# One bank tile for the pairs of heads, kept for the whole kernel, and a state update that writes 48 rows for each head

## The chip, the cores and the metric

The kernel runs on one core of one Trainium2 chip. The metric is the device time of one execution in microseconds (us), the median of several runs. For the kernel before, three runs took 460.72, 461.08 and 461.09 us, so the median is 461.08 us.

## The reference: what is computed

A gated linear attention feeds a feed-forward block that has no nonlinearity but one product. Cut to what matters:

```python
# q, k, v, f_logit: (batch 4, heads 8, sequence 768, head size 48), float32
f = 1.0 / (1.0 + np.exp(-f_logit))
for t in range(S):
    state = f[:, :, t, :, None] * state + np.einsum('bhd,bhe->bhde', k[:, :, t], v[:, :, t])
    y[:, :, t] = np.einsum('bhd,bhde->bhe', q[:, :, t], state)
x = y.transpose(0, 2, 1, 3).reshape(B * S, H * D)      # 3072 x 384
a = x @ w1                                             # 384 x 1024
b = x @ w2
h = a * b @ w3                                         # 1024 x 1024
out = h @ w_out                                        # 1024 x 384
```

## The kernel before, in words

The attention works on 24 units u of 128 positions (`C` = 128), six to each batch entry. The eight heads stand in four pairs hp. In the tiles of q, k and the gates the even head of a pair (par 0) has partitions 0 to 47 and the odd head (par 1) partitions 64 to 111. Partitions 48 to 63 between them are padding. The memsets in `setup` make the padding of q and k zero. `rows(par)` is the slice of 48 partitions of one head; `R` is 112, both heads with the padding between.

For each unit VectorE scans the gates forward (L529) and backward (L551) and scales q (L545) and k (L559). Scaled k is turned on TensorE (`turn`, L596) and copied to the tile `kt` by ScalarE (L730). From unit 2 on (`NPE` = 2) the units are cut into two halves of 64 positions (`W`), and the work of a unit on TensorE is this:

- `pairs` (L582): products of k and q, 16 matmuls of 64 x 64 outputs, into the left half (256 columns) of each of the two banks of the tile `pa`.
- `update` (L689): the product of turned k and v, which is what the unit adds to the state. For each pair hp, each half and each par there is one matmul, 16 in all, with 64 positions as the contraction and 48 columns of v as the moving operand. They write columns 256 to 447 of the two banks of the same `pa`, the first half's sums into bank 0 and the second's into bank 1. For par 0 the stationary operand has 64 columns of `kt` (head and padding), for par 1 it has 48 (`w` in L688), so that rows 0 to 111 are written without a gap. The last unit of each batch entry (u = 5, 11, 17, 23) does the first half alone, 8 matmuls.
- `values` (L656) and `from_state` (L675): the outputs of the unit, into `py`.

From unit 4 on (`SOLO` = 4) these are interleaved in one visit of TensorE, the function `visit` in `rest`: half of the values of unit u, the pairs of u + 1, the other half of the values, the part from the state of u, and last the update of u + 1. What reads `pa`: ScalarE copies the pairs (L706), GpSimd masks the copy in place (L712), and VectorE reads rows 0 to 111 of the update (L760, L762 and L765, the function `middle`) to make the state after each half. Of the state only the 48 rows of each head are used (L676, L677).

`pa` comes from the pool `ps`, which has one buffer for each name. `pairs` asks for the tile in each unit, so each unit's `pa` is a new tile at the old place, and its first write waits for everything that touched the tile before it.

Around the visits the same TensorE queue runs the products of weights and the feed-forward block: L901, L997, L1152 and L1470, 128 x 128 stationary operands with 192 to 384 columns moving. `idle` (L402) puts in matmuls without use. The order on every engine is set when the program is built: class `Plan` lists the tasks by written-out costs, due times and a limited number of banks, and the tasks are emitted in that order. The costs in the plan are not touched by the change. At run time each engine takes its instructions in that order and waits on semaphores.

Of the kernel before, what the change touches and what calls it, by code (L numbers as in the profile page):

```python
# [36 lines left out]
F32 = mybir.dt.float32  # L37
# [7 lines left out]
B, H, S, D = 4, 8, 768, 48  # L45
P = 128
# [13 lines left out]
NQ = HP * C  # L60
# [9 lines left out]
W = C // 2  # L70
# [220 lines left out]
def rows(par):  # L291
    return slice(64 * par, 64 * par + D)
# [3 lines left out]
def ranged(ctx, tc, q, k, f_logit, v, w1, w2, w3, w_out, out, ident, w12, wc, left):  # L296
# [15 lines left out]
    ps = pairing.enter_context(tc.tile_pool(name="ps", bufs=1, space=PSUM))  # L312
# [48 lines left out]
    found = {}  # L361
# [202 lines left out]

    def pairs(u):
        s = st[u]
        s["pa"] = ps.tile([P, 2, NQ], F32, name="pa")
        if u < NPE:
            for hp in range(HP):
                cols = slice(hp * C, hp * C + C)  # L570
                for par in range(2):
                    nc.tensor.matmul(
                        s["pa"][:, par, cols], lhsT=s["K"][rows(par), cols], rhs=s["Q"][rows(par), cols],
                        start=True, stop=True,
                    )
            return

        for hp in range(HP):
            for half in range(2):
                cols = slice(hp * C + half * W, hp * C + half * W + W)  # L580
                for par in range(2):
                    nc.tensor.matmul(  # L582
                        s["pa"][half * W : half * W + W, par, hp * W : hp * W + W],
                        lhsT=s["K"][rows(par), cols], rhs=s["Q"][rows(par), cols], start=True, stop=True,
                    )
# [94 lines left out]
    def update(u):  # L680

        s = st[u]
        s["pd"] = [s["pa"][0:R, half, HP * W : HP * W + HP * D].rearrange("p (h d) -> p h d", d=D) for half in range(2)]
        for hp in range(HP):
            for half in range(1 if u % NCH == NCH - 1 else 2):
                for par in range(2):
                    h = 2 * hp + par
                    w = 64 if par == 0 else D  # L688
                    nc.tensor.matmul(  # L689
                        s["pd"][half][64 * par : 64 * par + w, hp],  # L690
                        lhsT=s["kt"][half * W : half * W + W, hp, 64 * par : 64 * par + w],
                        rhs=s["v"][half * W : half * W + W, h * D : h * D + D], start=True, stop=True,
                    )

# [45 lines left out]
    def begin(u):  # L740

        def emit():
            pairs(u)
            update(u)

        t = tk[u]
        t["a"] = t["s"] = plan.add(
            "PE", 1.1, emit, [t["q"], t["k"], t["e"], t["lv"]] + past(u, 1, "m", "d"), need(u) - 999, slack=0.8,
        )
        paired(u)  # L750
# [20 lines left out]
    def rest(u):  # L771
        s, t = st[u], tk[u]
        opens, closes = u % NCH == 0, u % NCH == NCH - 1
        n0 = need(u)
        if u < NPE:
            t["a"] = plan.add("PE", 1.1, lambda: pairs(u), [t["q"], t["k"]] + past(u, 1, "m"), n0 - 1000)
            turning(u)
            paired(u)
# [6 lines left out]
        else:  # L785
# [4 lines left out]
            def visit():  # L790
                s["py"] = ps.tile([P, 2, NQ], F32, name="py")
                values(u, 1)
                if more:
                    pairs(u + 1)
                values(u, 0)
                from_state(u)
                if more:
                    update(u + 1)
# [822 lines left out]
    for item in EARLY:  # L1621
        if item in "ABCD":
            half, which = divmod("ABCD".index(item), 2)
# [394 lines left out]
```

## Time and profile before

| | before |
|---|---|
| median of three runs | 461.08 us |
| lowest and highest run | 460.72 and 461.09 us |
| span of the profiled execution, first to last instruction | 459.2 us |
| DVE (VectorE) busy in it | 370.7 us (81%) |
| ACT (ScalarE) busy | 211.7 us (46%) |
| POOL (GpSimd) busy | 66.3 us (14%) |
| DMA mean rate | 150 GB/s |
| granted TensorE clock | 1.000 |

The page gives the profiled execution's own time as its span alone, 459.2 us. It is 1.9 us under the median of the runs, which take in what lies ahead of the first instruction and behind the last. TensorE has two rows in the profile: PE is the matmuls, PEld the weight loads that run beside them. A 32-bit matmul of this kernel leaves two records of each (a transpose one), so 16 matmuls stand as x32. In a form such as `64*48 64x48` the first pair is the stationary operand (64 rows of contraction, 48 columns) and the second the moving one (64 rows, 48 columns). A line such as L689 is a line of the kernel; "f", "l", "pa" and "py" are banks. A releaser behind an arrow is what ended the idle time ahead of an instruction. "PEldq" and "PEq" are TensorE's sequencer, which passes the instructions on.

### The profile page before, as it was taken

What the parts mean: (1) busy time and instruction counts of PE and PEld (TensorE: products, weight loads), DVE (VectorE), ACT (ScalarE), POOL (GpSimd) and SP (SyncE); (2) the same over time, 40 slices, a digit from 0 to 9 for tenths busy, and PEclk for the clock granted to TensorE, in tenths of its full rate; (3) what the DMA queues carried; (4) which work ended last, traced back from release to release, by engine and by line L of the source; (5) the groups of instructions that cost most, each with busy time, mean ns of one, the idle gap of its engine ahead of it and who ended that gap; (6) DMA issues with size and microseconds to landing.
All of it is one profiled execution on the core that took longest, in us unless ns stands there. A gap on an engine that the chain in (4) does not pass through costs nothing.

```text
span 459.2 us, 11789 instructions
## 1 busy us (share of the span) xinstructions
PE 450.8 (98%) x4792; PEld 394.6 (86%) x4792; DVE 370.7 (81%) x651; ACT 211.7 (46%) x473; POOL 66.3 (14%) x90
## 2 busy tenths in 40 slices
PE   7999999999999999999999999999999999999996
PEld 6788886666899888889999888899899988889996
DVE  8997899999898999989999699896659466767641
ACT  3565344332233453543322256665665666665300
POOL 9331000121222531132222000000000000000000
PEclk9999999999999999999999999999999999999999
DMA  6997898833236664356322602436365522333111
GB/s 180 283 314 239 299 334 299 264 110 104 71 90 196 198 192 128 105 158 177 98 76 63 164 0 93 137 119 211 132 199 177 192 72 93 92 93 91 36 68 40
DMA packets 43309, 68.75 MB, mean 150 GB/s; under 512 B 5217, under 2 KB 28386, under 8 KB 42226
## 3 DMA queue, kind: packets, MB, share of 16 engines
q1 hardware_dynamic: 43250, 67.95, 48.2%
q8 instruction: 39, 0.64, 0.6%
q14 instruction: 20, 0.16, 0.1%
HBM read 58.88 MB, written 9.04 MB: 148 GB/s over the span
## 4 chain that ended last, share of the span: by engine, by line
PE 95%; DVE 1%; SPq 1%; DMA 1%; issue 0%; POOL 0%; POOLq 0%; DVEq 0%
PE f L901 24%; PE l L1152 15%; PE f L997 13%; PE f L1152 12%; PE f L1470 9%; PE l L901 9%; PE py L656 3%; PE pa L582 2%; PE pa L689 2%; PE f L596 2%; PE py L675 2%; PE f L402 1%; SPq L495 1%; DMA ab<-in_k_dram 1%; DVE K L559 0%
## 5 line engine op out<-in xcount | busy, mean ns | idle before, releaser
L712 POOL TENSOR_SCALAR_AFFINE_SELECT A<-A 64x512 f32<-64x512 f32 (+1 forms) x46 | 43.9, 955 | 110.5 <-ACT A L706 108.3
L1470 PE MATMUL f<-place 128*128 128x384 f32 x128 | 42.4, 487 | 0.0
L901 PE MATMUL f<-xt,w 128*128 128x256 f32 x192 | 42.1, 380 | 0.0
L901 PEld LDWEIGHTS f<-xt,w 128*128 128x128 f32 x192 | 36.3, 190 | 5.0
L1470 PEld LDWEIGHTS f<-place 128*128 128x128 f32 x128 | 23.9, 190 | 15.5
L901 PE MATMUL f<-place 128*128 128x192 f32 x176 | 31.9, 327 | 0.0
L997 PE MATMUL f<-xt,w 128*128 128x256 f32 x120 | 31.3, 380 | 0.0
L529 DVE TENSOR_TENSOR_SCAN fwd<-gate,floor 112x512 f32<-112x512 f32 x24 | 30.0, 1251 | 1.3 <-ACT gate L521 0.3
L551 DVE TENSOR_TENSOR_SCAN bwd<-gate,back 112x512 f32<-112x512 f32 x24 | 30.4, 1267 | 0.7
L901 PEld LDWEIGHTS f<-place 128*128 128x128 f32 x176 | 28.9, 190 | 0.4 <-issue 0.2
L848 ACT ACTIVATE ys<-py 112x512 f32<-112x512 f32 x22 | 13.1, 596 | 33.3 <-PE py L675 31.5
L997 PEld LDWEIGHTS f<-xt,w 128*128 128x128 f32 x120 | 22.5, 190 | 2.9
L901 PE MATMUL f<-wc,ab 128*128 128x192 f32 x128 | 23.6, 328 | 0.0
L1406 ACT ACTIVATE place<-place 128x512 f32<-128x512 uint32 (+2 forms) x24 | 21.2, 885 | 4.6 <-DMA place<-in_w_dram 4.0
L812 POOL TENSOR_TENSOR G<-lasts,gate 112x4 f32<-112x4 f32 x20 | 11.7, 586 | 75.1 <-ACT lasts L534 30.4
L901 PEld LDWEIGHTS f<-wc,ab 128*128 128x128 f32 x128 | 21.2, 190 | 0.3
L521 ACT ACTIVATE gate<-f 112x512 f32<-112x512 f32 x22 | 13.9, 632 | 16.0 <-DMA f<-in_f_logit_dram 7.0
L901 PE MATMUL l<-place 128*128 128x192 f32 x112 | 19.8, 326 | 0.0
L656 PEld LDWEIGHTS py<-A,vt 64*64 64x64 f32 (+1 forms) x672 | 13.3, 127 | 7.3 <-issue 6.5
L997 PE MATMUL f<-place 128*128 128x256 f32 x72 | 19.1, 386 | 0.0
L901 PEld LDWEIGHTS l<-place 128*128 128x128 f32 x112 | 18.5, 190 | 0.1
L656 PE MATMUL py<-A,vt 64*64 64x64 f32 (+1 forms) x672 | 18.0, 223 | 0.2
(288 smaller groups left out, 1066.7 us busy)
## 6 DMA issues: line engine op xcount, KB each, us to landing
place<-in_w_dram SPq DMA_DIRECT2D x21, 512.0 KB, 5.4
A<-in_w_dram SPq DMA_DIRECT2D x19, 512.0 KB, 4.0
place<-in_w_dram SPq DMA_DIRECT2D x8, 1024.0 KB, 6.2
q<-in_q_dram SPq DMA_DIRECT2D x46, 96.0 KB, 2.7
vt<-in_v_dram SPq DMA_DIRECT2D x23, 192.0 KB, 3.2
out_dram<-o SPq DMA_DIRECT2D x23, 192.0 KB, 2.9
k<-in_k_dram SPq DMA_DIRECT2D x44, 96.0 KB, 2.4
yt<-ys SPq DMA_DIRECT2D x44, 96.0 KB, 2.7
```

Source lines behind the costliest of these rows:

```text
L521: nc.scalar.activation(gate[u % 2][:, 0:NQ], fu, AF.Sigmoid)
L529: nc.vector.tensor_tensor_scan(s["P"], gate[u % 2][:, 0:NQ], floor, 0.0, ALU.mult, ALU.max)
L551: nc.vector.tensor_tensor_scan(s["R"][:, ::-1], gate[u % 2][:, NQ:0:-1], back[:, ::-1], 0.0, ALU.mult, ALU.max)
L656: done = nc.tensor.matmul(y_block(u, hp, par, half)[p0 : p0 + w], lhsT=s["v"][half * W : half * W + W, h * D : h * D + w], rhs=s["A"][half ...
L712: nc.gpsimd.affine_select(out=a, in_=a, pattern=pattern, compare_op=ALU.is_ge, fill=0.0, base=0, channel_multiplier=-1,)
L812: nc.gpsimd.tensor_tensor(s["G"], lasts[:, u], heads(gate[(u + 1) % 2][:, 0:NQ])[:, :, 0], ALU.mult)
L848: nc.scalar.activation(ys, py, AF.Copy, accum_out=ysum[:, u : u + 1])
L901: nc.tensor.matmul(out_, lhsT=lhs[i], rhs=rhs[i], start=start and i == 0, stop=i == len(lhs) - 1, skip_group_check=True,)
L997: nc.tensor.matmul(q[nm][:, which * TH : which * TH + TH], lhsT=lhs[i](which), rhs=rhs[i], start=start and which == 0 and i == 0, stop=i = ...
L1152: nc.tensor.matmul(banks[g, c][:, which * TH : which * TH + TH], lhsT=lhs, rhs=x_node(a), start=first and which == 0, stop=True, skip_grou ...
L1406: nc.scalar.activation(part_.bitcast(F32), part_, AF.Copy, bias=2.0, scale=2.0**-51)
L1470: nc.tensor.matmul(w3s["p", jc], lhsT=w3s[jc][:, kc * P : kc * P + P], rhs=wos[:, kc], start=(kc == 0), stop=(kc == KF - 1),)
```

## The change

It does two things. The tile `pa` is asked for once, in the first unit, and kept in `found`; all later units write to that one tile. And `update` takes `rows(par)` for both heads: the stationary operand has 48 columns for par 0 too, and rows 48 to 63 of `pa` are not written by the update any more. They keep what the pairs of the first two units left there, which filled all 128 rows; VectorE's reads of rows 0 to 111 go on as they were.

```diff
     def pairs(u):
         s = st[u]
-        s["pa"] = ps.tile([P, 2, NQ], F32, name="pa")
+        if "pa" not in found:
+            found["pa"] = ps.tile([P, 2, NQ], F32, name="pa")
+        s["pa"] = found["pa"]
...
                 for par in range(2):
                     h = 2 * hp + par
-                    w = 64 if par == 0 else D
                     nc.tensor.matmul(
-                        s["pd"][half][64 * par : 64 * par + w, hp],
-                        lhsT=s["kt"][half * W : half * W + W, hp, 64 * par : 64 * par + w],
+                        s["pd"][half][rows(par), hp],
+                        lhsT=s["kt"][half * W : half * W + W, hp, rows(par)],
                         rhs=s["v"][half * W : half * W + W, h * D : h * D + D], start=True, stop=True,
```

The order of the work on every engine stays; line numbers from 567 on move by two, and from 689 on by one. What moves is shown at two places. The first is TensorE's queue at the pairs and the update of unit 3 (the sizes here are those of the output, rows x columns; the name behind "waits" is the engine whose semaphore is waited for). Before:

```order
L675 MATMUL py<-Q,A 48x64 x7
L582 MATMUL pa<-Q,K 64x64 [waits DVE_49,PE_49]
L582 MATMUL pa<-Q,K 64x64 x15
L689 MATMUL pa<-place,kt 64x48 [waits DMAHW6_49,Activation_49]
L689 MATMUL pa<-place,kt 48x48
L689 MATMUL pa<-place,kt 64x48
L689 MATMUL pa<-place,kt 48x48
```

Twelve more rows of the update follow, 64 and 48 rows high by turns. The same place after the change:

```order
L677 MATMUL py<-Q,A 48x64 x7
L584 MATMUL pa<-Q,K 64x64 [waits DVE_49]
L584 MATMUL pa<-Q,K 64x64 x15
L690 MATMUL pa<-place,kt 48x48 [waits DMAHW6_49,Activation_49]
L690 MATMUL pa<-place,kt 48x48 x15
```

All 16 matmuls of the update are now 48 rows high, and the pairs no longer wait for TensorE's own earlier write of the tile. In 13 units such a wait goes; where it was the second wait of an instruction it had a sequencer instruction of its own, and 12 of these go from TensorE's queue.

The second place is ScalarE's copy of the pairs in the same unit. Before:

```order
L848 ACTIVATE ys,ysum<-py 112x2x2x128 [waits PE_49]
L1406 ACTIVATE place<-place 128x512 [waits DMAHW2_49]
L706 COPY A<-pa 128x512 [waits PE_49,Pool_49]
```

After the change:

```order
L849 ACTIVATE ys,ysum<-py 112x2x2x128 [waits PE_49]
L1407 ACTIVATE place<-place 128x512 [waits DMAHW2_49]
L707 COPY A<-pa 128x512 [waits DVE_49,PE_49,Pool_49]
```

Seven such copies now also wait for a VectorE instruction, the read of the update one unit earlier (L765 before). For four of them that takes one more sequencer instruction on ScalarE. VectorE, GpSimd and the DMA queues have the same instructions and the same waits as before.

## The prediction

> **What bounds the kernel now.** First the page: the busy shares, and the chain of work that ended last, by engine.
>
> ```profile
> PE 450.8 (98%) x4792; PEld 394.6 (86%) x4792; DVE 370.7 (81%) x651; ACT 211.7 (46%) x473; POOL 66.3 (14%) x90
> PE 95%; DVE 1%; SPq 1%; DMA 1%; issue 0%; POOL 0%; POOLq 0%; DVEq 0%
> ```
>
> TensorE is busy for 98% of the span and carries 95% of the chain, so what TensorE no longer does is a gain unless it then waits. The view of PE's waits is short:
>
> ```profile
> engine line waited for: us in total, times, longest us
> PE f L402 <- DVE floor L425: 1.7, 1, 1.7
> PE py L596 <- DVE K L559: 0.7, 1, 0.7
> PE pa L689 <- issue: 0.6, 1, 0.6
> PE f L596 <- DVE K L559: 0.4, 1, 0.4
> ```
>
> None of these lies in the long middle or in the feed-forward at the end. Now one visit in the timeline (start, length, engine, line, operation, shape, records):
>
> ```profile
> 146.95 0.56 PEld L582 LDWEIGHTS pa<-Q,K 48*64 48x64 f32 x32
> 147.64 0.31 PEld L675 LDWEIGHTS py<-Q,S 48*48 48x48 f32 x16
> 147.87 0.31 PEld L675 LDWEIGHTS py<-Q,A 48*48 48x48 f32 x16
> 148.09 0.56 PEld L689 LDWEIGHTS pa<-vt,kt 64*48 64x48 f32 x32
> 148.14 0.64 PE L689 MATMUL pa<-vt,kt 64*48 64x48 f32 x32
> 148.71 0.62 PEld L901 LDWEIGHTS f<-place,ab 128*128 128x128 f32 x4
> ```
>
> The update takes 0.62 us from its first weight load (148.09) to that of the next full-width matmul (148.71). The timeline names a merged group by its first shape; both widths are in it. So the decisive view is the groups with shapes kept apart, from 40 to 260 us, which holds the updates of units 4 to 23 (busy time is the union of the records; mean ns of one):
>
> ```profile
> L689 PE MATMUL pa<-vt,kt 64*64 64x48 f32 x288 | 12.4, 216 | 0.0
> L689 PE MATMUL pa<-vt,kt 64*48 64x48 f32 x288 | 11.0, 206 | 0.0
> L689 PEld LDWEIGHTS pa<-vt,kt 64*64 64x64 f32 x288 | 10.9, 135 | 0.0
> L689 PEld LDWEIGHTS pa<-vt,kt 64*48 64x48 f32 x288 | 9.4, 120 | 0.0
> ```
>
> The two widths are the same number of matmuls, with the same 64 rows of contraction and the same 48 columns moving, and they run side by side on the two column halves of the array. The wide ones take longer as a stream. That they also end later is seen in a window just ahead of the next full-width matmul, from 148.69 to 148.70, in which one group alone is left:
>
> ```profile
> L689 PE MATMUL pa<-vt,kt 64*64 64x48 f32 x4 | 0.3, 218 | 0.0
> ```
>
> So the 64-wide stream sets the end of the update, and the change makes it 48 wide.
>
> **The change part by part.** *Width of the update.* The 288 records of a width are 16 updates of 16 and four of 8, 20 updates. The streams differ by 12.4 - 11.0 = 1.4 us in matmuls and 10.9 - 9.4 = 1.5 us in loads: 0.07 to 0.075 us for each update. I take 0.075, as the stream of loads is what paces them (the moving operand is equal), so 20 x 0.075 = 1.5 us. The shorter last matmul (206 against 216 ns) is within the union and isn't counted again.
>
> This price assumes that two 48-wide streams run as fast as one beside a 64-wide one, which the trace doesn't show. From below: the nearest rows with 48 x 48 on all tiles are the two L675 groups, 16 matmuls from 147.64 to 147.87 + 0.31 = 148.18, or 0.54 us of loads against the update's 0.56; that would be 0.02 us each (their moving operand has 64 columns, which is why I don't take it). From above: the window shows the narrow stream over by 148.69 and the wide one ends at 148.14 + 0.64 = 148.78, at least 0.09 us later; I bound it by 0.10. A loss has no instruction to come from, since the counts are equal.
>
> The Trainium skill ("TensorE: Matmul & The Clock Gate", section "LDWEIGHTS (loading the stationary operand)") says that a weight load's time goes with its columns, columns / 1.2 in ns. An estimate from that page: 53 against 40 ns, 13 ns for each of eight loads in a row on a tile, 0.107 us an update, 2.3 us for 22 updates, 458.7 us. The rows have 135 against 120 ns, a difference of 15 ns, and agree in sign and about in size; the streams themselves show less, and I keep to them.
>
> *Units 2 and 3.* Unit 3's update stalls in its middle:
>
> ```profile
> 28.61 0.27 PE L689 MATMUL pa<-place,kt 64*48 64x48 f32 x3
> 29.47 0.67 PE L689 MATMUL pa<-place,kt 64*48 64x48 f32 x29 [0.59 <-issue]
> 208.16 0.78 PE L689 MATMUL pa<-vt,kt 64*48 64x48 f32 x32
> q8 instruction: 39, 0.64, 0.6%
> ```
>
> Nothing that the profile shows is waited for there. The 39 packets of instructions on q8 against 4792 + 4792 TensorE records make some 246 instructions a packet, so I read it as TensorE waiting for its own code. Unit 17's update (208.16) lasts 0.14 us longer than the one above, a small one of the kind. What unit 2 saves (at 23 us) runs into the large stall, whose end the code sets: 0. The rest of unit 3's update comes behind it: 0.075 us.
>
> *The waits that go.* The waits on TensorE's own write each had 51 ns of the sequencer:
>
> ```profile
> L582 PEldq EVENT_SEMAPHORE  x11: 51/51/51, 27.9 to 247.9; - x11
> L582 PE MATMUL pa<-Q,K 48*64 48x64 f32 x640 | 12.9, 218 | 0.0
> ```
>
> The matmuls of the pairs had no idle time ahead of them from 40 to 260 us (the 0.0 at the end): the write waited for is a whole unit old, and the sequencer runs ahead of the array behind the values. I take 0; the other end is 11 x 0.051 = 0.56 us.
>
> *The waits that come.* Four more sequencer instructions on ScalarE at most 0.2 us, on an engine 46% busy. Behind the copy stand ScalarE's later instructions and GpSimd's mask, for which the next visit's L656 waits. The closest case that I find:
>
> ```profile
> 158.93 1.53 POOL L712 TENSOR_SCALAR_AFFINE_SELECT A<-A 64x512 f32<-64x512 f32 x1
> 161.39 0.45 PE L656 MATMUL py<-A,vt 64*64 64x64 f32 x16
> ```
>
> The mask ended at 160.46, 0.93 us ahead of its use. The VectorE read that is newly waited for belongs to the unit before, and the pairs themselves still wait for VectorE to be past it, so it costs 0. Without that cover it would be 0.05 us four times.
>
> *Does the gain run into another wait?* TensorE gets up to 1.6 us ahead by unit 23. Its tightest wait after 40 us is on sums of VectorE:
>
> ```profile
> 124.67 0.42 DVE L943 TENSOR_TENSOR ab<-f,ab 128x256 f32<-128x256 f32 x1 [0.91 <-PE f L901]
> 125.86 0.69 DVE L1268 TENSOR_TENSOR place<-place,ab 128x512 f32<-128x512 f32 x1
> 126.70 1.54 PE L901 MATMUL f<-place 128*128 128x192 f32 x8
> ```
>
> TensorE starts 0.15 us after the sum. But that chain began with VectorE waiting 0.91 us for TensorE, so it moves along. The other close one is scaled k (L559) ahead of its turning:
>
> ```profile
> 168.54 0.69 DVE L559 TENSOR_TENSOR K<-k,bwd 112x512 f32<-112x512 f32 x1
> 169.99 0.60 PE L596 MATMUL f<-ident,K 112*128 112x112 f32 x4
> 167.48 0.69 DVE L1047 TENSOR_TENSOR a<-f,a 128x512 f32<-128x512 f32 x1 [0.22 <-PE f L997]
> ```
>
> There are 0.76 us to spare against the 0.8 us that eleven updates have gained by then. Were VectorE bound by itself, some 0.1 us would be lost here; but it had waited for TensorE a microsecond before, so it moves along. After 260 us the chain is TensorE's matmuls alone, so the lead is carried to the end.
>
> **The sum.** 1.5 + 0.075 = 1.6 us off the span: 459.2 - 1.6 = 457.6. The median of the runs is 1.9 us above the span and I keep that: 461.1 - 1.6 = **459.5 us**.
>
> **The rivals.** *Equal pace.* The narrow stream was quick only as the wide one left it the sequencer; two narrow ones go at the pace of L675, 0.02 us an update. Time: 461.1 - 21 x 0.02 = 460.7. For it: pairs and update, of different shapes, both show 0.56 us of loads. Against it: different limits can give that, 64 moving columns there and 64 weight columns here, and the groups of 12.4 and 11.0 us differ only in width. Chance 0.14. The Trainium skill ("TensorEngine Tiling (Array Packing)", section "Instruction Overhead") has a rule on this side: about 60 cycles for each matmul, one with a single moving column lasting as long as one with 60. By it a matmul with 48 moving columns stands on the floor already, and fewer weight columns give nothing: 461.1 us. The 206 against 216 ns and the shorter stream speak against it, and I leave it within this rival.
>
> *A code stall takes part of it.* With 12 sequencer instructions fewer, what stands at the edge of a code packet shifts by up to 12 instructions, and a visit can meet an edge that it missed before. One such stall of the size seen (28.61 to 29.47 less the normal pace, some 0.8 us) gives 459.5 + 0.8 = 460.3. For it: one visit of the early ones does it now. Against it: 12 of some 246 is a small shift, and the packets come far ahead in the slow stretches. Chance 0.10.
>
> *The other side: several code stalls.* The same mechanism in several visits, 0.8 us each, where visits are the densest code. Two take back the 1.6 us, and from the third on the kernel is slower: 461.9 us, with four 462.7. For it the one large and one small stall seen; against it that the other updates run through. Chance 0.04.
>
> That the change doesn't do what it says isn't open: the instructions are 48 wide.
>
> **How the numbers follow.** Forecast 0.72, equal pace 0.14, one stall 0.10, several 0.04. The range: the price of an update from 0.10 us for 22 of them (2.2 us, 458.9) down to 0.02 for 21 (460.7); it holds the forecast, one stall and the upper half of equal pace. A measurement of this kernel can tell about 0.2% from no change, 0.92 us, so "faster" is under 460.16. Faster: the forecast and what of the others falls under it, 0.72 + 0.05 = 0.77. Slower needs over 462.0, four stalls: 0.03. The rest, 0.20, is the same.
>
> **What would show it.** Right: one form of L690, 64*48, 16 matmuls in some 0.54 us from first load to the next full-width load, where 0.62 stood; 0.07 to 0.08 us off each visit, no new PE waits beyond 0.1 us, the span near 457.6. Wrong: the update still near 0.6 us though narrower (equal pace); a new "issue" wait in a visit (code); a wait of L596 or L901 for VectorE that eats the lead.

## The result, and the profile after

| | before | after |
|---|---|---|
| median of four runs each | 461.07 us | 458.59 us |
| lowest and highest | 460.72 and 461.09 | 458.04 and 458.81 |
| span of the profiled execution | 459.2 us | 456.2 us |

The ratio is 0.9949, with a 95% interval of 0.9935 to 0.9963. The time fell by 2.5 us; the forecast was 1.6 us, and 458.59 lies 0.3 us below the range. The profiled execution of the changed kernel is the 458.04 us one.

The page of the changed kernel: busy shares, the chain by engine, and the packets of instructions.

```profile
PE 448.7 (98%) x4792; PEld 392.5 (86%) x4792; DVE 371.1 (81%) x651; ACT 212.0 (46%) x473; POOL 69.1 (15%) x90
PE 95%; DVE 1%; SPq 1%; DMA 1%; POOL 0%; issue 0%; POOLq 0%; DVEq 0%
q8 instruction: 38, 0.62, 0.6%
```

TensorE has the same number of matmuls and weight loads and carries the chain as before; it is busy for 2.1 us less (450.8 to 448.7). The view of PE's waits:

```profile
PE f L402 <- DVE floor L425: 1.7, 1, 1.7
PE py L598 <- DVE K L559: 0.5, 1, 0.5
PE f L598 <- DVE K L559: 0.5, 1, 0.5
```

The waits for VectorE at the start are where they were, no new one has come, and the 0.6 us of "issue" in the update is gone. Now the visit of the prediction in the timeline of the weight loads: second part from the state, update, next full-width load.

```profile
146.40 0.31 PEld L677 LDWEIGHTS py<-Q,A 48*48 48x48 f32 x16
146.62 0.47 PEld L690 LDWEIGHTS pa<-vt,kt 64*48 64x48 f32 x32
147.15 0.19 PEld L902 LDWEIGHTS f<-place,ab 128*128 128x128 f32 x1
```

All 32 loads of the update are 64*48 now. They last 0.47 us where they lasted 0.56, and the next full-width load comes 0.53 us after the first of them, where it came 0.62 us after. The groups with shapes kept apart, from 38 to 258 us, show it for units 4 to 23 together:

```profile
L690 PE MATMUL pa<-vt,kt 64*48 64x48 f32 x576 | 10.8, 205 | 0.0
L690 PEld LDWEIGHTS pa<-vt,kt 64*48 64x48 f32 x576 | 9.3, 121 | 0.0
```

Here both streams are in one group, and their union is 9.3 us of loads, where the wide stream alone had 10.9 and the narrow one alone 9.4.

The lead is the time by which the changed kernel is ahead. How it grew is read from the same load in both traces: the first one after unit 3's update, and the first one after unit 23's. Before (unit 2's update and the start of unit 3's stand ahead, for what follows):

```profile
22.65 0.55 PEld L689 LDWEIGHTS pa<-vt,kt 64*64 64x64 f32 x32
23.25 0.20 PEld L596 LDWEIGHTS f<-ident,K 112*128 112x128 f32 x2
...
28.55 0.20 PEld L689 LDWEIGHTS pa<-place,kt 64*48 64x48 f32 x3
29.47 0.54 PEld L689 LDWEIGHTS pa<-place,kt 64*48 64x48 f32 x29 [0.71 <-issue]
30.06 0.30 PEld L402 LDWEIGHTS f<-floor 112*128 112x128 f32 x2
...
249.90 0.30 PEld L997 LDWEIGHTS f<-xt,w 128*128 128x128 f32 x2
```

After:

```profile
28.41 0.68 PEld L690 LDWEIGHTS pa<-place,kt 64*48 64x48 f32 x32
29.15 0.30 PEld L402 LDWEIGHTS f<-floor 112*128 112x128 f32 x2
...
246.99 0.30 PEld L998 LDWEIGHTS f<-xt,w 128*128 128x128 f32 x2
```

The lead is 0.91 us behind unit 3 and 2.91 us behind unit 23: 2.00 us in 20 updates. Of the 0.91 us most is the stall in unit 3's update, 0.9 us before (1.51 us to the next group, from its first load at 28.55, where unit 2's took 0.60) and here about 0.2 (0.68 us of loads where others have 0.47). The small stall that the prediction found in "unit 17's update" is gone too. It lies in the update of unit 18, which TensorE does in the visit of unit 17: unit 17's own update is the half one before it. After the change:

```profile
205.96 0.54 PE L690 MATMUL pa<-vt,kt 64*48 64x48 f32 x32
```

This update was 0.78 us, 0.14 more than the other wide ones. Without that the 20 updates gave 1.86 us, 0.093 each.

### The profile page after: what moved, and what is told of

It reads as the page before. It is cut to its first block, busy times and chain, and to the rows that moved or that the text cites. A ratio compares the mean times of both kernels' runs of the same rounds, so it can differ in the third digit from the quotient of the medians.

```text
span 456.2 us, 11781 instructions
## 1 busy us (share of the span) xinstructions
PE 448.7 (98%) x4792; PEld 392.5 (86%) x4792; DVE 371.1 (81%) x651; ACT 212.0 (46%) x473; POOL 69.1 (15%) x90
## 4 chain that ended last, share of the span: by engine, by line
PE 95%; DVE 1%; SPq 1%; DMA 1%; POOL 0%; issue 0%; POOLq 0%; DVEq 0%
PE f L902 25%; PE l L1153 15%; PE f L998 13%; PE f L1153 12%; PE f L1471 9%; PE l L902 9%; PE py L658 3%; PE pa L584 2%; PE f L598 2%; PE py L677 2%; PE pa L690 2%; PE f L402 1%; SPq L495 1%; DMA ab<-in_k_dram 1%; DVE K L559 0%
## 5 line engine op out<-in xcount | busy, mean ns | idle before, releaser
L713 POOL TENSOR_SCALAR_AFFINE_SELECT A<-A 64x512 f32<-64x512 f32 (+1 forms) x46 | 46.2, 1004 | 107.8 <-ACT A L707 105.7
```

Source lines behind the costliest of these rows:

```text
L713: nc.gpsimd.affine_select(out=a, in_=a, pattern=pattern, compare_op=ALU.is_ge, fill=0.0, base=0, channel_multiplier=-1,)
```

## The experiments

**Theory 1:** each of 22 updates is 0.093 us shorter because the wide stream set its end; this is 2.05 us, and what goes beyond it are stalls of TensorE's code, which vary by themselves. **Theory 2:** a part comes from the waits that went. Runs of different groups were made on different chips, so each is compared with the kernel before in its own rounds.

### One half of the change alone

```diff
-        s["pa"] = ps.tile([P, 2, NQ], F32, name="pa")
+        if "pa" not in found:
+            found["pa"] = ps.tile([P, 2, NQ], F32, name="pa")
+        s["pa"] = found["pa"]
```

> Only the first half of the change: one bank tile for all units, the update still 64 columns wide for par 0. Theory 1 (the width is what shortens each update by 0.094 us, 0.618 to 0.524 from its first load to the next full-width load): every update from unit 4 on still takes 0.62 us, no visit is shorter, and the time differs from the kernel before only by the code stalls of units 3 and 17, at most 0.9 us: 460.1 to 461.1. Theory 2 (the waits that go are worth a part, 51 ns of the sequencer at 12 places): visits with a removed wait are 0.05 us shorter and the time is 460.4 even with the stalls as before.

Measured: median 460.70 us against 460.57 before, ratio 1.0012 (0.9991 to 1.0033). The timeline of the loads in the same visit, and of the matmuls in unit 3:

```profile
148.28 0.31 PEld L677 LDWEIGHTS py<-Q,A 48*48 48x48 f32 x16
148.51 0.56 PEld L691 LDWEIGHTS pa<-vt,kt 64*48 64x48 f32 x32
149.12 0.30 PEld L903 LDWEIGHTS f<-place,ab 128*128 128x128 f32 x2
...
28.56 0.27 PE L691 MATMUL pa<-place,kt 64*48 64x48 f32 x4
29.78 0.66 PE L691 MATMUL pa<-place,kt 64*64 64x48 f32 x28 [0.95 <-issue]
```

The update is 0.56 us of loads and 0.61 us to the next full-width load, as before, though the wait is gone. Unit 3's stall is even longer. From the first load of unit 4's update to that of unit 23's this kernel takes 163.96 us, the kernel before 164.00 with the 0.14 us of unit 18's stall in it, and the changed kernel 162.10. So Theory 2 falls for the time in the visits. The other half alone, the width with a new tile for each unit, was not tried: the rows between the heads would be read without ever having been written.

### The width with the waits put back

```diff
     def pairs(u):
...
+        if "last" in found:
+            ordered(nc.tensor.nop(), found["last"])
...
-                    nc.tensor.matmul(
+                    found["last"] = nc.tensor.matmul(
                         s["pd"][half][rows(par), hp],
```

> The changed kernel with the wait for TensorE's own last update put back ahead of every unit's pairs (17 sequencer instructions more than the changed kernel, 5 more than the kernel before). Theory 1: the updates stay at 0.52 us and the time within 0.2 us of the changed kernel, but for code stalls: 458.0 to 459.5. Theory 2: 0.05 us is lost at up to 13 places, 0.6 us, 459.2.

Measured: median 460.13 us against 460.57, ratio 0.9990 (0.9975 to 1.0004), outside what both theories expected. The loads in the visit, and the one new wait in the trace:

```profile
147.42 0.47 PEld L692 LDWEIGHTS pa<-vt,kt 64*48 64x48 f32 x32
147.94 0.19 PEld L904 LDWEIGHTS f<-place,ab 128*128 128x128 f32 x1
...
165.08 0.92 PE L1000 MATMUL f<-xt,place 128*128 128x256 f32 x3 [0.96 <-issue]
```

The visits have the whole gain (0.47 and 0.52 us) with the waits in place. From the first load of unit 4's update to that of unit 12's both this kernel and the changed one take 76.71 us, so the waits cost nothing where they stand. What eats the gain in the profiled execution is above all a stall of 1 us in the feed-forward (165.08) and one of 0.9 us in unit 3. In the DMA records a 16 KB packet of code ended at 163.61 us, 1.47 us ahead of the stall's end; for unit 3 of the first profile of the kernel before it ended at 28.00, 1.47 us ahead of 29.47. The likely reading is that the 17 instructions have moved the code against the edges of its packets; the next run tests it.

### Is it code? Shifting it

```diff
-    plan.add("PE", 7.8, lambda: idle(9), prio=-1e8)
+    plan.add("PE", 7.8, lambda: idle(18, TH // 2), prio=-1e8)
```

(`idle` takes the width as a second argument here.)

> The changed kernel with the first nine matmuls without use (256 columns) made into 18 of 128 columns: the same time there, and 36 instructions more in TensorE's queue, so that all later code lies 36 instructions further on. If the stall of unit 3 is TensorE waiting for its next 16 KB of code, it moves to 36 instructions (nine matmuls) earlier in the program, into the pairs of unit 3 (L584), and the updates keep their 0.52 us. If the stall belongs to the update (a wait for its operands), it stays at the same matmul of L690.

Measured, one run: 458.23 us against 460.55. The loads of unit 3:

```profile
28.04 0.43 PEld L584 LDWEIGHTS pa<-Q,K 48*64 48x64 f32 x19
28.70 0.26 PEld L584 LDWEIGHTS pa<-Q,K 48*64 48x64 f32 x11 [0.22 <-issue]
```

The stall has left the update and stands in the pairs, after 19 loads. In the unshifted kernel it came after 4 loads of the update, which is 32 + 4 = 36 loads after the first of the pairs: 17 loads earlier, and with a load and a matmul for each that is 34 instructions, near the 36 put in. So it belongs to a place in the code, not to the update. Here too a packet had ended shortly before, at 27.27 us, 1.43 us ahead of 28.70.

### The second profiles

> The kernel before once more, for a second profile. If the stall in unit 3 is a matter of when the code packet comes in that execution, it lies anywhere between the 0.14 and 1.16 us seen in six profiles of other kernels, and unit 17's may be gone. If the kernel fixes it, it is again 0.8 us in unit 3 and 0.14 us in unit 17. The updates take 0.62 us either way.

Measured, one run: 460.52 us. Unit 3's loads, then unit 18's matmuls (the expectation's "unit 17"):

```profile
28.64 0.66 PEld L689 LDWEIGHTS pa<-place,kt 64*48 64x48 f32 x32
29.35 0.30 PEld L402 LDWEIGHTS f<-floor 112*128 112x128 f32 x2
...
207.44 0.84 PE L689 MATMUL pa<-vt,kt 64*48 64x48 f32 x32
```

In unit 3 this execution of the same kernel lost 0.1 us (0.71 us from first load to the next group, against 0.60 of its like, unit 2's), where the first had lost 0.9. So the size of unit 3's stall is not the kernel's. Unit 18's stall has come again (0.84 us, 0.20 more than the other wide ones). It is in both profiles of the kernel before and not in that of alloc_only, which has the changed kernel's count of sequencer instructions: 43 ahead of this update, where the kernel before has 53. Nor is it in layout_before (further down), which has all 53 and only lies 152 instructions further on:

```profile
207.40 0.64 PE L694 MATMUL pa<-vt,kt 64*48 64x48 f32 x32
```

So this stall, too, belongs to a place in the code, and the 10 instructions fewer have moved it away.

> The changed kernel once more, for the spread. Width theory: 22 updates shorter by 0.094 us, 2.07 us in all, and no more than that on average: about 2.1 us below the median of the kernel before in the same rounds (0.9955), and 0.52 us for each update again. If the stall that the first comparison lost in unit 3 (0.8 us) were gone for good by the change, 2.5 to 3.0 us (0.994).

Measured: median 458.63 us against 460.55, ratio 0.9965 (0.9953 to 0.9976): 1.9 us. Its loads:

```profile
147.29 0.47 PEld L690 LDWEIGHTS pa<-vt,kt 64*48 64x48 f32 x32
147.81 0.30 PEld L902 LDWEIGHTS f<-place,ab 128*128 128x128 f32 x2
...
28.95 0.44 PEld L690 LDWEIGHTS pa<-place,kt 64*48 64x48 f32 x28 [0.33 <-issue]
```

The updates are as in the first profile, and unit 3 stalled longer than there (0.49 us over its like's 0.47 of loads, against 0.21). The 2.5 us of the first comparison were not all the change's.

### What paces a stream now

The changed kernel with less work in the update, in three ways: 32 columns of the stationary operand, 32 of the moving one, 32 of both.

```diff
-                        lhsT=s["kt"][half * W : half * W + W, hp, rows(par)],
+                        lhsT=s["kt"][half * W : half * W + W, hp, 64 * par : 64 * par + 32],
```

```diff
-                        rhs=s["v"][half * W : half * W + W, h * D : h * D + D],
+                        rhs=s["v"][half * W : half * W + W, h * D : h * D + 32],
```

The slice of `pa` that is written is cut to match.

> The changed kernel with the update's stationary operand cut to 32 columns for each head; the rows 32 to 47 of each head's state are left out. What paces a stream now? If the weight load alone (13 ns for each 16 columns and 8 loads in a row), the update goes from 0.524 to 0.42 us. If the longer of load and moving operand, both 48 columns now, it stays within 0.02 us of 0.524, and the time at about 458.5.

> The changed kernel with 32 of the 48 columns of v moving in the update and the stationary operand left at 48, so that the array keeps its division into 64 x 64; the columns 32 to 47 of each head's state are left out. If the longer of load and moving operand sets the step, it stays at 45 ns and the update at 0.52 us. If the moving operand sets it now, the step falls to about 32 ns and the update to 0.42 us.

> The changed kernel with 32 columns of the stationary operand and 32 of the moving one in the update; of each head's 48 x 48 state only 32 x 32 is computed. If the longer of the two sets the pace, the step falls from 45 to 32 ns and the update from 0.524 to about 0.43 us; if the pace of issue sets it, it stays above 0.48 us.

Measured, one run each: 461.00, 457.77 and 458.44 us. The loads of the same visit, narrow32, moving32 and both32 in turn:

```profile
147.78 0.31 PEld L677 LDWEIGHTS py<-Q,A 48*48 48x48 f32 x16
148.17 0.41 PEld L690 LDWEIGHTS pa<-vt,kt 64*32 64x32 f32 x32
148.65 0.19 PEld L902 LDWEIGHTS f<-place,ab 128*128 128x128 f32 x1
```

```profile
146.59 0.47 PEld L690 LDWEIGHTS pa<-vt,kt 64*48 64x48 f32 x32
147.10 0.19 PEld L902 LDWEIGHTS f<-place,ab 128*128 128x128 f32 x1
```

```profile
146.66 0.31 PEld L677 LDWEIGHTS py<-Q,A 48*48 48x48 f32 x16
147.05 0.34 PEld L690 LDWEIGHTS pa<-vt,kt 64*32 64x32 f32 x32
147.44 0.30 PEld L902 LDWEIGHTS f<-place,ab 128*128 128x128 f32 x2
```

Fewer moving columns alone leave the loads at 0.47 us; fewer columns of weights alone bring them to 0.41, and both together to 0.34. By the records of this visit the loads of one tile come 58 ns apart with 64 columns of weights (before), 45 ns in the changed kernel and in moving32, 42.5 in narrow32 and 32 in both32. That is what the longer of load and moving operand would give, and at 48 x 48 the two are nearly level. moving32 kept 0.51 us from its first load to the next full-width one, as that theory has it, and both32 came down to 0.39. But the two kernels with 32 columns of weights lose elsewhere: their first load of the update comes 0.39 us after the first of the last state group, where it was 0.22 us (146.40 to 146.62). From that group to the next full-width load narrow32 takes 0.87 us, against 0.75 for the changed kernel and 0.84 for the kernel before. From the first load of unit 4's update to that of unit 23's narrow32 takes 164.40 us, the changed kernel 162.10. So narrow32 fits neither of its two expectations: its update, from its first load to the next full-width one, took 0.48 us, between the 0.42 of the one and the 0.50 or more of the other, and its time is not 458.5 us.

### A version without the stall, and one that goes further

The first nine matmuls without use became 47 of 32 x 46 outputs, 152 instructions more ahead of all other code; in the kernel before, in the changed one, and in one that also cuts `values` to 48 columns.

```diff
-    plan.add("PE", 7.8, lambda: idle(9), prio=-1e8)
+    def short(n):
+        to = ps_f.tile([P, TB], F32, name=f"f{NF - 1}")[0:32, 0:46]
+        for _ in range(n):
+            nc.tensor.matmul(to, lhsT=floor[:, 0:32], rhs=floor[:, 0:46], start=True, stop=True)
+
+    plan.add("PE", 7.8, lambda: short(47), prio=-1e8)
```

> The kernel before, with the first nine matmuls without use (128 x 256 outputs) replaced by 47 of 32 x 46 outputs in about the same time: 152 instructions more ahead of the rest of TensorE's code, so that no 16 KB edge falls into unit 3's visit and none just ahead of another visit. If the stall in unit 3 (0.81 us in the first profile) is code that comes late, it goes: 0.3 to 0.8 us below the kernel before, about 459.9. If it is anything else of that visit, it stays.

> The changed kernel with the same 47 short matmuls. With no code stall in either, the two differ by the width alone: 22 x 0.094 = 2.07 us below layout_before. Against the changed kernel itself 0.1 to 0.4 us less (the stall left in unit 3 was 0.14 and 0.41 us in its two profiles): about 458.3.

The matmuls of unit 3 in the two, and what the changed one does next:

```profile
28.46 0.63 PE L694 MATMUL pa<-place,kt 64*48 64x48 f32 x32
29.02 1.13 PE L402 MATMUL f<-floor 112*128 112x256 f32 x4
```

```profile
28.50 0.53 PE L695 MATMUL pa<-place,kt 64*48 64x48 f32 x32
28.96 1.13 PE L402 MATMUL f<-floor 112*128 112x256 f32 x4
30.51 0.89 PE L907 MATMUL f<-xt,w 128*128 128x256 f32 x3 [0.42 <-DVE w L1437]
```

The stall is gone in both. (By the 0.47 us of its like's loads the stall left in the changed kernel was 0.21 and 0.49 us in its two profiles, not the 0.14 and 0.41 of the expectation.) In this group the kernel before had 460.79 us, layout_before 460.10 (ratio 0.9988, 0.9978 to 0.9997) and layout_after 458.16 (0.9939, 0.9926 to 0.9952). The width is worth 460.10 - 458.16 = 1.94 us between two kernels whose profiles show no stall in unit 3, which agrees with 2.05 within the spread of the runs. In its profiled execution layout_after also waited 0.42 us for weights that VectorE makes, once the code came in time; whether that took a part of the gain isn't shown, and the profile of layout_values48 doesn't have this wait.

The cut in `values`, alone and with the shifted code:

```diff
-                w = 64 if hp < 2 else D
+                w = 64 if hp < 2 and u == NPE else D
...
-                s["py"] = ps.tile([P, 2, NQ], F32, name="py")
+                if "py" not in found:
+                    found["py"] = ps.tile([P, 2, NQ], F32, name="py")
+                s["py"] = found["py"]
```

> The changed kernel, and the same cut made in the function values: 48 columns for all heads from unit 3 on, with the tile py kept as well. There 64 columns are loaded and 64 are moving, so a step goes from 58 ns only to the 55 ns of the moving operand: 3 ns x 4 steps x 2 halves = 0.024 us a visit, 0.5 us in 21 visits, 458.0. If the load alone set the step it would be 13 ns a step, 0.1 us a visit, 2.2 us. If values are hidden beside the pairs, nothing.

> The kernel with 48 columns in values as well, with the same 47 short matmuls: 0.3 to 0.5 us below layout_after, about 457.9, and the fastest of all.

Measured: values48 458.20 us against 460.55 before and 458.63 for the changed kernel in the same rounds, ratio to before 0.9959 (0.9946 to 0.9972). layout_values48 457.76 us against 460.79 before and 458.16 for layout_after, ratio 0.9936 (0.9921 to 0.9951). Both medians are some 0.4 us lower, but the intervals overlap. The traces are steadier: from the first load of unit 4's update to that of unit 23's the changed kernel takes 162.10 and 162.15 us and layout_after 162.09, while both kernels with the cut take 161.77. That is 0.33 us in 19 visits, 0.017 us each where 0.024 was expected of the 55 ns of the moving operand. Of all kernels run layout_values48 has the lowest median.

## Why the prediction was right or wrong

*What bounds the kernel: right.* TensorE's busy time fell by 2.1 us and the profiled span by 3.0. The other 0.9 us is idle time that went, 0.6 of it in the stall of unit 3.

*The wide stream sets the end of the update: right.* alloc_only keeps 0.56 us of loads, the changed kernel has 0.47, waits_back too.

*The price of an update: too small, and this is the first of two steps that failed.* "I take 0.075" was the loads of the wide stream less those of the narrow one beside it, 10.9 - 9.4 us. The 9.4 us held 0.13 us of the code stall in unit 18. In alloc_only, which is without that stall, the same rows from 40 to 260 us are:

```profile
L691 PEld LDWEIGHTS pa<-vt,kt 64*64 64x64 f32 x288 | 10.9, 135 | 0.0
L691 PEld LDWEIGHTS pa<-vt,kt 64*48 64x48 f32 x288 | 9.3, 120 | 0.0
```

Their difference makes 0.08 us an update. And the narrow stream was slower in the wide one's company: by the load records of a full visit it lasted 0.468 us there, and the later of the two narrow streams of the changed kernel, which takes the wide one's place, lasts 0.454. The two together make 0.094 us. Measured 0.093 us for each update, 22 x 0.093 = 2.05 us against the 1.6 of the sum. The upper bound that I gave, 0.10 for each, held it. The estimate from the Trainium skill ("TensorE: Matmul & The Clock Gate", section "LDWEIGHTS (loading the stationary operand)"), 0.107 us an update, was nearer than my row; it is 0.014 over.

*Equal pace, the rival at 0.02 us: wrong.* Two narrow streams have 9.3 us of loads together, as one has alone in alloc_only; both32 shows that even 0.34 us of loads an update can be issued. The Trainium skill's floor of about 60 cycles for a matmul, by which one moving column lasts as long as 60 ("TensorEngine Tiling (Array Packing)", section "Instruction Overhead"), doesn't hold for the pace of these: with 32 columns of weights, 48 against 32 moving columns make 0.41 and 0.34 us of loads (narrow32 and both32).

*The waits that go: 0 in the visits, right; but not in all.* waits_back and alloc_only show no time at the waits. The changed kernel's 10 instructions fewer ahead of unit 18's update moved a code edge, which was worth 0.14 and 0.20 us in the two profiles of the kernel before. I had let the shift of code only cost, not gain. The rival of one code stall did not come true in the changed kernel, but its mechanism did in waits_back: 0.96 us in the feed-forward.

*The stall of unit 3: the second step that failed, and the one that put the time outside the range.* With 2.05 us for the width alone the median would have been 459.0 us, inside it. I took the stall's end as fixed, so that unit 2's gain was lost in it and nothing else changed, and the range had no term for a stall that shrinks. In the ten profiles other than those of shift36 and the three layout kernels it varied from 0.1 to 1.3 us, and both kernels that were profiled twice showed two sizes. The first comparison gained from it: its profiles differ by 0.7 us there, and with the width's 2.05 and unit 18's 0.14 us that makes 2.9 of the 3.0 us between their spans. That, and the spread of the kernel before (medians of 460.55 to 461.07 us on the occasions it was timed), is the likely reason why 2.5 us were measured first and 1.9 when repeated. How much of the first 2.5 was luck can't be told run by run, since only one execution of each group has a profile.

*The lead runs into no other wait: right* in the changed kernel. In layout_after, with more lead at 30 us, one did come, for the weights that VectorE makes.

*The added waits on ScalarE: right at 0.* No wait of TensorE for the mask has come into its list.

## What to carry to other kernels

When two streams of matmuls run side by side on parts of the array, the slower one sets the end and can slow the other, so price the cut from the step of a load (here 58 to 45 ns, seven steps in a row), not from how long the faster stream lasted in its company. Load no padding columns: where the moving operand isn't longer, each costs time even when the result is thrown away. With code as dense as these visits, a few instructions more or less can move a stall of a microsecond, so compare two layouts of the code before a tenth of a per cent is believed.

## What the runs showed of the hardware

- **A group with 32 columns of weights behind one with 48 started 0.17 us later.** In narrow32 and both32 the update's first load waited until 0.39 us after the first of the group ahead, against 0.22 us; moving32, with 48 columns of weights, had no such delay. The Trainium skill ("TensorEngine Tiling (Array Packing)", section "Key Properties") says that a change of tiling mode drains TensorE. That this is the cause here was not tested by itself. The delay is more than 16 columns fewer gain here (0.06 us of loads).
- **Code arrives in packets of 16 KB, and TensorE can run out of it.** The changed kernel has 38 such packets, 0.62 MB. In the cases set side by side above the stall ended 1.43 to 1.47 us after the packet did. It moved when 36 instructions were put ahead, and in unit 3 it left when 152 were. Why the same packet comes up to a microsecond earlier or later in different executions was not tried; the weights are being loaded at that time (a DMA share of 0.81 in the first 30 us of the kernel before), which may be the reason.
